# Attention and top-1 experts on one core: the first two pairs transposed on TensorE, a second token buffer, the gates' products moved to the score buffers

## The chip, the cores and the metric

The kernel runs on one core of one Trainium2 chip. The metric is the device time of one execution in microseconds. Before the change it was 905.83 us, the median of three runs (904.97 to 908.14).

## The reference

```python
scores = (q @ k.T) / sqrt(D) - log(S)          # per batch and head; B=8, H=12, S=448, D=64
attn   = sigmoid(scores) @ v
x      = attn, heads beside each other         # 3584 tokens x 768
logits = x @ w_gate                            # 768 x 8
expert = argmax(logits); gate = softmax(logits)[expert]
out    = gate * (relu(x @ w1[expert]) @ w2[expert])   # w1 768x1024, w2 1024x768
```

Everything is float32. The kernel splits the operands of the experts into a high and a low fp32r part and adds three products (high x high, high x low, low x high).

## The kernel before

**Attention** works on pairs of heads, six to a batch, 48 in all; two pairs run side by side, in seven steps each, which makes 168 steps. `scores(s)` puts the products of two pairs into two of four PSUM buffers (tag `sc`), `squash` turns each into `at` on ScalarE, and `weighted` adds the products with v into `av`, two buffers of its own. A pair's keys and queries are loaded by `load_pair` as 32 x 32 blocks and transposed by VectorE in `turn`, in the steps that `READY` names. The first two pairs are loaded and turned ahead of the loop, after `warm_up(WARM)`, 76 small matmuls on a constant.

**Experts.** When a batch's attention is done, its gate finds each token's expert and the expert that most of the batch's tokens chose. That expert is run over the whole batch as a block: `moe(b)` makes 288 matmuls, 144 with w1 (L208) into eight sums, then 144 with w2 (L229) into six, each sum in one of two PSUM buffers (tag `moe`). `hh` (ScalarE) and `hl` (VectorE, L214) are the two parts of a w1 sum after the relu; `ob` (L237, VectorE, then a multiplication by the gate on POOL, L239) is the transposed w2 sum. The weights are loaded by SP into a ring of five buffers (tag `wst`); ScalarE makes the high part and POOL subtracts it (`w1l`, `w2l`, L144).

**The interleaving.** One generator, `attention()`, goes through 185 steps and yields twice in each; from step `START` (33) on, each yield is followed by seven expert matmuls. So the order of the instructions on each engine is the order of the code. Two matmul steps of attention stand together in every even step, ahead of the first yield. In the second part of a step stands what the gate of the batch before has to do:

- a: `gate_a`, the product with the gate weights (`psg`), copied to `g16`
- b: four small transposes (`pl`), then a chain of VectorE operations to the one-hot rows `oh`
- c: the count of tokens for each expert (`pc`), then the expert's number and the gate values
- l: SP reads the expert's number into a register, from where the block's weights can be loaded
- d: the prefix sums (`pr`), VectorE's chain to the row numbers `si`, and four indirect DMAs of records on POOL (L355), for the tokens that chose another expert
- e: the gate values in rows (`gm`, `pg`, `gt`), needed at the block's first L239
- tokens: in six further steps, VectorE adds the two parts of x into `xf` (L398) and transposes it into `xt` (L399); after the third and the sixth, SP writes `xt` to `x_tok` with four DMAs (L403)

Steps a to e stand on neighbouring steps, with the exception that batch 0 has one free step behind b. The products psg, pl, pc, pr and pg are taken from `small_ps`, which shares the two `moe` buffers with the experts' sums. `xt` has one buffer.

**The tail.** After the loop, VectorE makes the list of the remaining work items (experts with records of other batches), `pli` (L675) turns it, and two loops with hardware counters run over the items. Between the parts of that list, `more(8)` puts eight of the last expert matmuls each. In an item, `AT` says after which matmul each split of the next item's weights is put.

Of the kernel before, what the change touches and what calls it, by code (L numbers as in the profile page):

```python
# [10 lines left out]
F32 = mybir.dt.float32  # L11
# [14 lines left out]
def tile_sigmoid_attention_top1_moe(  # L26
# [363 lines left out]
    def tokens(b, t):  # L390

        NB = S // 32
        n, t = divmod(t, KH)
        if t == 0:
            xts[b] = xtpool.tile([P, NB, KH, 32], F32, tag="xt", bufs=1, name=f"xt_{b}_{n}")
        xf = xtpool.tile([P, S], F32, tag="xf", bufs=1, name=f"xf_{b}_{n}_{t}")
        xh, xl = xch[b, n * KH + t]
        nc.vector.tensor_add(xf, xh.bitcast(F32), xl.bitcast(F32))  # L398
        nc.vector.transpose(xts[b][:, :, t, :], xf.rearrange("p (j s) -> p j s", s=32))  # L399
        if t == KH - 1:  # L400
            rows = x_tok[b * S : (b + 1) * S].rearrange("(j r) (i f) -> i r j f", r=32, i=4)
            for i in range(4):
                nc.sync.dma_start(  # L403
                    rows[i][:, :, n * KH * 32 : (n + 1) * KH * 32],
                    xts[b][32 * i : 32 * (i + 1)].rearrange("r j t s -> r j (t s)"),
                )

    def small_ps(b, name):

        return ps_moe.tile([P, 512], F32, tag="moe", name=f"{name}_{b}")  # L410

    att = ExitStack()
    xtpool = att.enter_context(tc.tile_pool(name="xtpool", bufs=2))
# [5 lines left out]

    DK = P // 2  # L420
    KC = S // DK
    ops = {}
    NG = B * NP
    OWN = [slice(h * D, (h + 1) * D) for h in range(2)]
# [5 lines left out]
    def load_pair(g):  # L430
        if g >= NG:
            return
        b, hp = divmod(g, NP)
        for nm, src in (("k", k), ("q", q)):
            t = apool.tile([P, S // 32, 32], F32, tag=nm + "n", bufs=4, name=f"{nm}n_{g}")
            eng = nc.scalar if g < Q_ACT and nm == "q" else nc.sync
            for h in range(2):
                for f in range(D // 32):
                    a = 2 * h + f
                    eng.dma_start(  # L440
                        t[32 * a : 32 * (a + 1)],
                        src[b, 2 * hp + h, :, 32 * f : 32 * (f + 1)].rearrange("(j r) s -> r j s", r=32),
                    )
            ops[g, nm + "n"] = t

    def load_values(g):
        if g >= NG:
# [16 lines left out]
    def warm_up(n):  # L464

        ps = ps_moe.tile([P, 512], F32, tag="moe", name="ps_warm")
        for _ in range(n):
            nc.tensor.matmul(ps[:, :P], ones, ones, start=True, stop=True)
# [4 lines left out]
    N_ST = NG // 2 * ST  # L473

    def squash(g, c, ps):
        at = apool.tile([P, S], F32, tag="at", bufs=10, name=f"at_{g}_{c}")
        nc.scalar.activation(at, ps[:, :S], AF.Sigmoid, bias=bias_s, scale=SCALE)  # L477
        ats[g, c] = at

# [32 lines left out]
                nc.vector.tensor_sub(xl, pv[:, :S], xh.bitcast(F32))  # L512
                xch[divmod(g, NP)] = (xh, xl)

    WARM, V_POOL, Q_ACT = 76, 10, 2
    START = 33
    PB = NP // 2 * ST
    MIX = (7, 7)

# [7 lines left out]
    def attention():  # L527

        order = ExitStack()
        order.enter_context(tc.manual_schedule())  # L530
        warm_up(WARM)
        load_pair(0)
        load_pair(1)
        for g in range(2):
            turn(g, "k")
            turn(g, "q")
            load_values(g)
        for g in (2, 3):
            load_pair(g)
# [3 lines left out]
        for s in range(N_ST + 11 + KD):  # L543
# [19 lines left out]
            if gb >= 0:  # L563
                b, r = divmod(gb, PB)
                r -= 3 if b == 0 else 2
                at = ("a", "b", None, "c", "l", "d", "e") if b == 0 else ("a", "b", "c", "l", "d", "e")
                what = at[r] if 0 <= r < len(at) else None
                if what == "a":
                    gate_a(b)
                elif what == "b":  # L570
                    pend_gate = gate_b(b)
                elif what == "c":
                    pend_gate = gate_c(b, *pend_gate)
                    gate_out[b] = pend_gate[0]
                elif what == "l":
                    load_regs(b)
                    if b == 0:
                        wts.ahead(0)
                elif what == "d":
                    gate_d(b, *pend_gate)  # L580
                elif what == "e":
                    gate_e(b)
                if 7 <= r < 7 + KD:
                    tokens(b, r - 7)
            yield s, MIX[1]
        order.close()

# [9 lines left out]
    def more(n):  # L597
        nonlocal left
        for _ in range(min(n, left)):
            next(mo)  # L600
            left -= 1
# [4 lines left out]
    for s, n in attention():  # L606
        if s >= START:
# [12 lines left out]
    AT = (  # L620
        (
            dict(zip((0, 1, 2, 3, 4, 12, 5, 6, 7, 8, 13, 14, 15, 16, 9, 10, 11, 17),
                     (33, 39, 45, 51, 57, 84, 102, 108, 114, 120, 126, 132, 138, 144, 150, 156, 162, 175))),
            (74, 90, 128, 168),
        ),
        (dict(zip((0, 1, 4, 5, 8, 9, 2, 3, 6, 7, 10, 11), (16, 20, 24, 28, 33, 42, 48, 54, 60, 66, 72, 78))), ()),
# [21 lines left out]
    nc.vector.tensor_scalar(cut(0), cut(0), float(P), None, op0=ALU.add)  # L648
    nc.vector.tensor_tensor(ek(4), ek(0), n_rec, op=ALU.is_lt)
    nc.vector.tensor_sub(few, few, big)  # L650
    more(8)
    for msk, cum in zip((big, few), rank):
        nc.vector.tensor_tensor_scan(cum, cut(3), msk, 0.0, op0=ALU.mult, op1=ALU.add)
    ends = rest.tile([P, 2], F32, name="ends")
# [2 lines left out]
    nc.vector.tensor_scalar(rank[1], rank[1], ends[:, 0:1], None, op0=ALU.add)  # L657
    for msk, cum in zip((big, few), rank):
        nc.vector.scalar_tensor_tensor(msk, cum, slot1, msk, op0=ALU.is_equal, op1=ALU.mult)
    more(8)  # L660
    nc.vector.tensor_add(big, big, few)
    prod = cut(8, 2).rearrange("p (a n) -> p a n", a=2)
    nc.vector.tensor_mul(
# [5 lines left out]
    ki = rest.tile([1, 2], I32, name="ki")  # L669
    nc.vector.tensor_scalar(ends[:, 0:1], ends[:, 1:2], -1.0, ends[:, 0:1], op0=ALU.add, op1=ALU.max)  # L670
    nc.vector.tensor_copy(ki, ends[0:1])
    more(8)
    pli = ps_x.tile([P, 512], F32, tag="px", name="pli")
    for a in range(2):
        nc.tensor.matmul(pli[0:1, a * P : (a + 1) * P], lf[:, a : a + 1], ident, start=True, stop=True)  # L675
# [237 lines left out]
```

## Time and profile before

| | before |
|---|---|
| median of three runs | 905.83 us |
| the profiled execution | 907.99 us |
| its span | 905.8 us |
| mean granted TensorE clock | 0.979 |
| TensorE (PE) busy | 859.9 us |
| VectorE, ScalarE, POOL busy | 376.4, 382.1, 413.5 us |
| bytes moved | 120.62 MB |

The times of the table's lower part belong to one profiled execution, on one core. The span goes from its first to its last recorded instruction. A group of instructions is written as engine, line, output <- inputs; a wait is put down to the instruction that ended it. These are the groups on which TensorE spends its time (busy us, mean ns of one, then idle time ahead of them and what ended it):

```profile
L503 PE MATMUL av<-at,vn 64*64 64x448 f32 x1344 | 157.8, 562 | 0.1
L490 PE MATMUL sc<-qt,kt 64*64 64x448 f32 x1344 | 152.2, 542 | 5.4 <-DVE qt L461 5.4
L208 PE MATMUL ps<-xh,w1h 128*128 128x448 f32 x384 | 144.2, 375 | 7.1 <-DVE hl L214 7.1
L229 PE MATMUL ps<-hh,w2h 128*128 128x448 f32 x384 | 143.6, 374 | 1.0 <-DVE g L260 1.0
```

### The profile page before, as it was taken

Reading aid. Unit: us, or ns where it says so; the run is one execution under the profiler, and the core shown is the slowest. Engines: PE = TensorE matmul, PEld = TensorE weight load, DVE = VectorE, ACT = ScalarE, POOL = GpSimd, SP = SyncE. Lnnn points to the kernel's source line nnn. Section 1 sums busy time; section 2 is a strip of 40 time slices with the busy share of each in tenths; the row PEclk is TensorE's granted clock in tenths of the full one; section 3 lists DMA queues with packets and bytes.
Section 4 is the critical chain, followed back from the end, with each engine's and each line's share of the span. In section 5 each row is a group of like instructions: output and inputs, shape, how many; then the busy total and the mean of one; then the engine's idle time right before and its main releaser. Section 6 shows DMA issues by size and latency. Waiting matters only on the chain.

```text
span 905.8 us, 15548 instructions
## 1 busy us (share of the span) xinstructions
PE 859.9 (95%) x5622; PEld 633.5 (70%) x5622; DVE 376.4 (42%) x729; ACT 382.1 (42%) x689; POOL 413.5 (46%) x377
## 2 busy tenths in 40 slices
PE   7989999999899999999999999999999999889986
PEld 4656766767577676677676676677676788779775
DVE  2356134732426225642434225532345136546354
ACT  3765434335243533354253543354344521324344
POOL 3115325823355415733475325732474358556240
PEclk8999999999999999999999999999999999999999
DMA  9878642876147843685248834676355306736614
GB/s 145 137 148 196 162 97 74 187 162 141 31 125 185 190 80 91 151 197 107 59 121 201 188 58 111 141 179 122 75 143 143 97 21 165 191 104 194 215 52 142
DMA packets 305644, 120.62 MB, mean 133 GB/s; under 512 B 215300, under 2 KB 300372, under 8 KB 305568
## 3 DMA queue, kind: packets, MB, share of 16 engines
q1 hardware_dynamic: 294368, 104.25, 49.8%
q0 software_dynamic: 7488, 14.93, 6.9%
q10 hardware_dynamic: 3712, 0.46, 0.4%
q8 instruction: 44, 0.72, 0.4%
q14 instruction: 32, 0.26, 0.1%
HBM read 97.55 MB, written 24.64 MB: 135 GB/s over the span
## 4 chain that ended last, share of the span: by engine, by line
PE 79%; DVE 7%; DMA 5%; POOL 3%; issue 2%; SPq 2%; ACT 1%; POOLq 0%; DVEq 0%; ACTq 0%
PE ps L208 23%; PE ps L229 22%; PE av L503 15%; PE sc L490 13%; PE ps L789 3%; PE psg L256 2%; DMA x_tok<-xt 1%; DMA qn<-in_q_dram 1%; DMA w2r<-in_moe_w_dram 1%; DVE xf L398 1%; POOL w1l L144 1%; DMA out_dram<-ob 1%; SPq L403 1%; DVE ob L237 1%; SPq L440 1%
## 5 line engine op out<-in xcount | busy, mean ns | idle before, releaser
L477 ACT ACTIVATE at<-sc,bias_s 128x448 f32<-128x448 f32 x336 | 187.1, 641 | 237.1 <-PE sc L490 236.8
L144 POOL TENSOR_TENSOR w2l<-wst,w2h 128x512 fp32r<-128x512 f32 x96 | 122.1, 1293 | 200.2 <-ACT w2h L143 153.3
L144 POOL TENSOR_TENSOR w1l<-wst,w1h 128x768 fp32r<-128x768 f32 x64 | 119.8, 1884 | 136.4 <-ACT w1h L143 129.7
L503 PE MATMUL av<-at,vn 64*64 64x448 f32 x1344 | 157.8, 562 | 0.1
L490 PE MATMUL sc<-qt,kt 64*64 64x448 f32 x1344 | 152.2, 542 | 5.4 <-DVE qt L461 5.4
L208 PE MATMUL ps<-xh,w1h 128*128 128x448 f32 x384 | 144.2, 375 | 7.1 <-DVE hl L214 7.1
L208 PE MATMUL ps<-xh,w1l 128*128 128x448 f32 x384 | 144.1, 375 | 1.9 <-POOL w1l L144 1.9
L229 PE MATMUL ps<-hh,w2h 128*128 128x448 f32 x384 | 143.6, 374 | 1.0 <-DVE g L260 1.0
L208 PE MATMUL ps<-xl,w1h 128*128 128x448 f32 x384 | 144.0, 375 | 0.0
L229 PE MATMUL ps<-hl,w2h 128*128 128x448 f32 x384 | 143.0, 372 | 0.0
L229 PE MATMUL ps<-hh,w2l 128*128 128x448 f32 x384 | 141.8, 369 | 0.0
L490 PEld LDWEIGHTS sc<-qt,kt 64*64 64x64 f32 x1344 | 77.1, 191 | 66.2 <-issue 55.4
L214 DVE SCALAR_TENSOR_TENSOR hl<-ps,hh 128x448 fp32r<-128x448 f32 x64 | 39.5, 617 | 183.6 <-ACT hh L213 183.6
L503 PEld LDWEIGHTS av<-at,vn 64*64 64x64 f32 x1344 | 49.5, 135 | 62.4 <-issue 52.1
L208 PEld LDWEIGHTS ps<-xh,w1h 128*128 128x128 f32 x384 | 73.7, 192 | 22.3 <-DVE hl L214 8.2
L229 PEld LDWEIGHTS ps<-hh,w2h 128*128 128x128 f32 x384 | 74.8, 195 | 15.6 <-issue 8.6
L208 PEld LDWEIGHTS ps<-xh,w1l 128*128 128x128 f32 x384 | 73.7, 192 | 16.2 <-issue 5.8
L208 PEld LDWEIGHTS ps<-xl,w1h 128*128 128x128 f32 x384 | 73.7, 192 | 14.0 <-issue 8.2
L229 PEld LDWEIGHTS ps<-hh,w2l 128*128 128x128 f32 x384 | 74.7, 195 | 11.4 <-issue 7.1
L229 PEld LDWEIGHTS ps<-hl,w2h 128*128 128x128 f32 x384 | 74.6, 194 | 9.8 <-issue 6.5
L143 ACT CAST w2h<-wst 128x512 fp32r<-128x512 f32 x96 | 57.6, 625 | 55.2 <-PE ps L229 51.0
L213 ACT ACTIVATE hh<-ps 128x448 fp32r<-128x448 f32 x64 | 35.2, 551 | 102.7 <-PE ps L208 102.7
(145 smaller groups left out, 891.4 us busy)
## 6 DMA issues: line engine op xcount, KB each, us to landing
wst<-in_moe_w_dram SPq DMA_DIRECT2D x64, 384.0 KB, 4.3
wst<-in_moe_w_dram SPq DMA_DIRECT2D x48, 512.0 KB, 4.6
kn<-in_k_dram SPq DMA_DIRECT2D x192, 56.0 KB, 3.9
x_tok<-xt SPq DMA_DIRECT2D x64, 168.0 KB, 3.9
out_dram<-ob POOLq DMA_DIRECT2D x96, 112.0 KB, 3.1
qn<-in_q_dram SPq DMA_DIRECT2D x184, 56.0 KB, 2.8
vn<-in_v_dram SPq DMA_DIRECT2D x76, 112.0 KB, 4.0
w1r<-in_moe_w_dram SPq DMA_DIRECT2D x12, 512.0 KB, 3.9
```

The source lines that it names most:

```text
L143: nc.scalar.copy(hi, st)
L144: eng.tensor_tensor(lo, st, hi.bitcast(F32), op=ALU.subtract)
L208: nc.tensor.matmul(ps[:, :S], a[:, ws], b_, start=(t == 0 and n == 0), stop=(t == KD - 1 and n == 2))
L213: nc.scalar.activation(hh[:, :S], ps[:, :S], AF.Relu)
L214: nc.vector.scalar_tensor_tensor(hl[:, :S], ps[:, :S], 0.0, hh[:, :S].bitcast(F32), op0=ALU.max, op1=ALU.subtract)
L229: nc.tensor.matmul(ps[:, :S], a, b_, start=(j == 0 and n == 0), stop=(j == KF - 1 and n == 2))
L237: nc.vector.transpose(ob[:, :, :, t], ps[:, :S].rearrange("p (j s) -> p j s", s=32))
L256: nc.tensor.matmul(psg[: 2 * E, :S], wgs[:, t], xch[b, t][n], start=(t == 0 and n == 0), stop=(t == KD - 1 and n == 1),)
L477: nc.scalar.activation(at, ps[:, :S], AF.Sigmoid, bias=bias_s, scale=SCALE)
L490: nc.tensor.matmul(ps[quarter(g, h), :S], ks, ops[g, "q"][OWN[h]], start=True, stop=True)
L503: nc.tensor.matmul(psv[g][OWN[h], :S], ops[g, "v"][rows, c, :], at[rows], start=(c == 0), stop=(c == KC - 1))
L789: nc.tensor.matmul(*a, **kw)
```

## The change

**First pairs.** `load_pair` isn't called for pairs 0 and 1. `first_pair` loads each as rows, 112 partitions of four tokens each, two DMAs for k (from SP) and two for q (from ScalarE's queue), into a buffer of the weights' ring. `first_turn` transposes it on TensorE, four transposes of 112 columns for each of k and q into a score buffer, and VectorE (k) or ScalarE (q) copies it out, with the tokens put back into their order. The two loads stand ahead of the warm-up, which has 50 matmuls instead of 76.

**Gates.** `small_ps` takes its buffer from the four score buffers. The steps are a, b, free, c, l, free, d, free, e for every batch, so a step for c, l and d of most batches and more for e lies later than before; the six token steps come one later.

**Token copies.** `xt` has two buffers; `at` has eight instead of ten.

**Start and tail.** `START` is 36 instead of 33. In the tail, three times 20 expert matmuls stand between the parts of the list instead of eight (the last `more(8)` stays), and the first five splits in `AT` stand three to five matmuls later.

```diff
@@ tokens @@
-            xts[b] = xtpool.tile([P, NB, KH, 32], F32, tag="xt", bufs=1, name=f"xt_{b}_{n}")
+            xts[b] = xtpool.tile([P, NB, KH, 32], F32, tag="xt", bufs=2, name=f"xt_{b}_{n}")
@@ small_ps @@
-        return ps_moe.tile([P, 512], F32, tag="moe", name=f"{name}_{b}")
+        return ps_sc.tile([P, 512], F32, tag="sc", name=f"{name}_{b}")
@@ load_pair @@
-            eng = nc.scalar if g < Q_ACT and nm == "q" else nc.sync
@@ new @@
+    PF = S // 4
+    def first_pair(g):
+        b, hp = divmod(g, NP)
+        t = wpool.tile([P, 1024], F32, tag="wst", bufs=RAWS_AHEAD, name=f"first_{g}")
+        tv = t[:PF].rearrange("p (n c h d) -> p n c h d", n=2, c=4, h=2)
+        for n, src in enumerate((k, q)):
+            for h in range(2):
+                eng = nc.scalar if n else nc.sync
+                eng.dma_start(tv[:, n, :, h], src[b, 2 * hp + h].rearrange("(p c) d -> p c d", c=4))
+        ops[g, "first"] = t
+
+    def first_turn(g):
+        t = ops.pop((g, "first"))
+        for n, nm in enumerate("kq"):
+            ps = score_tile(f"first_{g}_{nm}")
+            for c in range(4):
+                at = (4 * n + c) * P
+                nc.tensor.transpose(ps[:, c * PF : (c + 1) * PF], t[:PF, at : at + P], ident[:PF, :PF])
+            to = apool.tile([P, S], F32, tag=nm + "t", bufs=4, name=f"{nm}t_{g}")
+            tov, psv_ = to.rearrange("d (p c) -> d c p", c=4), ps[:, :S].rearrange("d (c p) -> d c p", c=4)
+            if nm == "k":
+                nc.vector.tensor_copy(tov, psv_)
+            else:
+                nc.scalar.copy(tov, psv_)
+            ops[g, nm] = to
@@ squash @@
-        at = apool.tile([P, S], F32, tag="at", bufs=10, name=f"at_{g}_{c}")
+        at = apool.tile([P, S], F32, tag="at", bufs=8, name=f"at_{g}_{c}")
@@ constants @@
-    WARM, V_POOL, Q_ACT = 76, 10, 2
-    START = 33
+    WARM, V_POOL = 50, 10
+    START = 36
@@ attention @@
+        for g in range(2):
+            first_pair(g)
         warm_up(WARM)
-        load_pair(0)
-        load_pair(1)
         for g in range(2):
-            turn(g, "k")
-            turn(g, "q")
+            first_turn(g)
             load_values(g)
...
-                at = ("a", "b", None, "c", "l", "d", "e") if b == 0 else ("a", "b", "c", "l", "d", "e")
+                at = ("a", "b", None, "c", "l", None, "d", None, "e")
...
-                if 7 <= r < 7 + KD:
-                    tokens(b, r - 7)
+                if 8 <= r < 8 + KD:
+                    tokens(b, r - 8)
@@ AT, first loop @@
-                     (33, 39, 45, 51, 57, 84, 102, 108, 114, 120, 126, 132, 138, 144, 150, 156, 162, 175))),
+                     (38, 43, 48, 54, 60, 84, 102, 108, 114, 120, 126, 132, 138, 144, 150, 156, 162, 175))),
@@ the list of items, three times @@
-    more(8)
+    more(20)
```

How the order of the instructions changes is seen at three places. First, TensorE after the warm-up (`sc_first_0_k` is the score buffer into which the keys of pair 0 are transposed; `sc_0_1` belongs to pair 0, step 1). Before:

```order
L468 MATMUL ps_warm_129<-ones_96 128x128
L490 MATMUL sc_0_0_261<-qt_0_228,kt_0_226 64x448 x2
L490 MATMUL sc_1_0_262<-qt_1_235,kt_1_233 64x448 x2
L490 MATMUL sc_0_1_271<-qt_0_228,kt_0_226 64x448 x2
L490 MATMUL sc_1_1_272<-qt_1_235,kt_1_233 64x448 x2
L503 MATMUL av_0_298<-at_0_0_267,vn_0_230 64x448 x2
```

After:

```order
L495 MATMUL ps_warm_139<-ones_96 128x128
L464 MATMUL sc_first_0_k_190<-ident_80,first_0_129 128x112 x4
L464 MATMUL sc_first_0_q_197<-ident_80,first_0_129 128x112 x4
L464 MATMUL sc_first_1_k_207<-ident_80,first_1_134 128x112 x4
L464 MATMUL sc_first_1_q_214<-ident_80,first_1_134 128x112 x4
L517 MATMUL sc_0_0_245<-qt_0_202,kt_0_195 64x448 x2
L517 MATMUL sc_1_0_246<-qt_1_219,kt_1_212 64x448 x2
L517 MATMUL sc_0_1_255<-qt_0_202,kt_0_195 64x448 x2
L517 MATMUL sc_1_1_256<-qt_1_219,kt_1_212 64x448 x2
L530 MATMUL av_0_282<-at_0_0_251,vn_0_204 64x448 x2
```

The last warm-up matmul is now followed by sixteen transposes in four buffers, and then by the same scores.

Second, POOL around the start of the last block, 7 (`ob_6_1` is the second output part of block 6, `w1l_7_0` the low part of block 7's first weights, `rec_7` the records of batch 7). Before:

```order
L144 TENSOR_TENSOR w2l_6_19_7759<-wst_6_13_7468,w2h_6_19_7758 128x512
L239 TENSOR_TENSOR ob_6_1_7644<-ob_6_1_7644,gt_6_7063 128x896
L244 DMA out_0_dram<-ob_6_1_7644 32x14x64 x4
L144 TENSOR_TENSOR w1l_7_0_7802<-wst_7_0_7777,w1h_7_0_7801 128x768
L351 IOTA rec_7_7831 128x4
L355 DMA recs_58<-rec_7_7831,si_7_7829 28672x2 x4
L144 TENSOR_TENSOR w1l_7_1_7852<-wst_7_1_7779,w1h_7_1_7851 128x768
```

After:

```order
L144 TENSOR_TENSOR w2l_6_19_7760<-wst_6_13_7480,w2h_6_19_7759 128x512
L351 IOTA rec_7_7787 128x4
L355 DMA recs_58<-rec_7_7787,si_7_7785 28672x2 x4
L239 TENSOR_TENSOR ob_6_1_7662<-ob_6_1_7662,gt_6_7084 128x896
L244 DMA out_0_dram<-ob_6_1_7662 32x14x64 x4
L144 TENSOR_TENSOR w1l_7_0_7818<-wst_7_0_7731,w1h_7_0_7817 128x768
L144 TENSOR_TENSOR w1l_7_1_7836<-wst_7_1_7733,w1h_7_1_7835 128x768
```

The records' four DMAs have moved from behind `ob_6_1`, its writes and `w1l_7_0` to a place ahead of all three.

Third, VectorE at the token copies of batch 7 (`xf_7_1_0` is the sum for the first of the second three, `hl_7_0` the low part of block 7's first two w1 sums). Before:

```order
L214 SCALAR_TENSOR_TENSOR hl_7_0_7931<-ps1_7_0_7907,hh_7_0_7930 128x448
L398 TENSOR_TENSOR xf_7_0_1_7944<-xh_43_7020,xl_43_7021 128x448
L399 STREAM_TRANSPOSE xt_7_0_7915<-xf_7_0_1_7944 128x14x32
L398 TENSOR_TENSOR xf_7_0_2_7961<-xh_44_7355,xl_44_7356 128x448
L399 STREAM_TRANSPOSE xt_7_0_7915<-xf_7_0_2_7961 128x14x32
L214 SCALAR_TENSOR_TENSOR hl_7_0_7931<-ps1_7_1_7940,hh_7_0_7930 128x448
L398 TENSOR_TENSOR xf_7_1_0_7992<-xh_45_7359,xl_45_7360 128x448
L399 STREAM_TRANSPOSE xt_7_1_7991<-xf_7_1_0_7992 128x14x32
L214 SCALAR_TENSOR_TENSOR hl_7_2_8001<-ps1_7_2_7977,hh_7_2_8000 128x448
```

After:

```order
L237 STREAM_TRANSPOSE ob_6_2_7809<-ps2_6_2_1_7848 128x448
L398 TENSOR_TENSOR xf_7_0_2_7906<-xh_44_7261,xl_44_7262 128x448
L399 STREAM_TRANSPOSE xt_7_0_7858<-xf_7_0_2_7906 128x14x32
L214 SCALAR_TENSOR_TENSOR hl_7_0_7925<-ps1_7_0_7898,hh_7_0_7924 128x448
L398 TENSOR_TENSOR xf_7_1_0_7939<-xh_45_7265,xl_45_7266 128x448
L399 STREAM_TRANSPOSE xt_7_1_7938<-xf_7_1_0_7939 128x14x32
L398 TENSOR_TENSOR xf_7_1_1_7956<-xh_46_7507,xl_46_7508 128x448
L399 STREAM_TRANSPOSE xt_7_1_7938<-xf_7_1_1_7956 128x14x32
L214 SCALAR_TENSOR_TENSOR hl_7_0_7925<-ps1_7_1_7934,hh_7_0_7924 128x448
```

The copies now stand further ahead: the second half's first two are in front of the second `hl_7_0`, where there was none before; `ob_6_2`, which was ahead of all of the copies, stands among them.

More of the change, by code (lines that the diff above doesn't have):

```diff
@@ L439, in load_pair @@
                     a = 2 * h + f
-                    eng.dma_start(
+                    nc.sync.dma_start(
                         t[32 * a : 32 * (a + 1)],
@@ L659, in tile_sigmoid_attention_top1_moe @@
         nc.vector.scalar_tensor_tensor(msk, cum, slot1, msk, op0=ALU.is_equal, op1=ALU.mult)
-    more(8)
+    more(20)
     nc.vector.tensor_add(big, big, few)
@@ L671, in tile_sigmoid_attention_top1_moe @@
     nc.vector.tensor_copy(ki, ends[0:1])
-    more(8)
+    more(20)
     pli = ps_x.tile([P, 512], F32, tag="px", name="pli")
```

## The prediction

> **What bounds the kernel.** I read the page first.
>
> ```profile
> PE 859.9 (95%) x5622; PEld 633.5 (70%) x5622; DVE 376.4 (42%) x729; ACT 382.1 (42%) x689; POOL 413.5 (46%) x377
> ```
>
> TensorE is busy for 860 of 905.8 us and no other engine for half. The change takes no expert or attention matmul away, so what it can win is TensorE's idle time and slow clock. The view of waits for PE gives the first:
>
> ```profile
> PE ps L208 <- DVE hl L214: 7.1, 3, 3.9
> PE sc L490 <- DVE qt L461: 5.4, 2, 5.1
> PE pg L378 <- DVE gm L374: 5.2, 5, 1.9
> PE pli L675 <- DVE lf L667: 4.0, 1, 4.0
> PE pc L302 <- DVE ob L237: 2.9, 2, 2.8
> ...
> PE ps L208 <- POOL w1l L144: 1.9, 1, 1.9
> ...
> PE pr L334 <- DVE pre L338: 1.1, 2, 0.5
> PE ps L229 <- DVE g L260: 1.0, 2, 0.5
> PE pc L302 <- DVE oh L289: 0.9, 1, 0.9
> PE pl L265 <- DVE g L260: 0.8, 1, 0.8
> PE pl L265 <- DVE ob L237: 0.5, 1, 0.5
> ```
>
> Columns: total us, times, longest. Nearly every wait is for VectorE, and nearly every one belongs to an edit. The second half of the price is the granted clock (the stretch, then busy times, then PEclk third from the end):
>
> ```profile
> 68.70:72.00 3.30, 3.30 (x24) 1.34 (x20) 3.23 (x6) 0.89 (x2) 2.39 (x4) 0.50 1.21 265
> 188.20:191.50 3.30, 3.30 (x11) 2.90 (x10) 3.27 (x7) 0.00 (x0) 1.57 (x1) 0.50 0.13 19
> 246.20:249.50 3.30, 3.30 (x18) 1.05 (x20) 2.19 (x11) 0.00 (x0) 2.89 (x5) 0.50 0.36 61
> 362.30:365.60 3.30, 3.30 (x16) 1.41 (x18) 0.00 (x0) 0.30 (x1) 2.67 (x4) 0.50 0.02 1
> 765.00:768.30 3.30, 3.30 (x11) 2.91 (x10) 3.30 (x1) 0.00 (x0) 3.00 (x3) 0.50 0.63 180
> 782.10:785.40 3.30, 3.30 (x11) 2.92 (x10) 1.44 (x3) 0.00 (x0) 0.00 (x0) 0.50 0.61 170
> 799.20:802.50 3.30, 2.96 (x9) 2.16 (x10) 0.98 (x4) 0.00 (x0) 0.00 (x0) 0.50 0.00 0
> ```
>
> Each of these 3.3 us stretches runs at half clock and lies just behind a wait. Sixteen attention matmuls show what one costs, cold and warm:
>
> ```profile
> 246.69 3.13 PE L503 MATMUL av<-at,vn 64*64 64x448 f32 x16
> ```
> ```profile
> 194.47 1.67 PE av L503 x16
> ...
> 197.64 5.86 PE ps L208 x28
> ...
> 206.67 5.86 PE ps L208 x28
> ```
>
> 3.4 x (1 - 1.67/3.13) = **1.6 us** a stretch. The same rows give an expert matmul 5.86/28 = 0.209 us, and a pair of steps with attention 206.67 - 197.64 = 9.03 us. Which waits pull the clock down:
>
> ```profile
> 67.95 0.28 PE L378 MATMUL pg<-gm,same 128*128 128x16 f32 x1 [1.64 <-DVE gm L374]
> ```
> ```profile
> 187.37 0.47 PE L208 MATMUL ps<-xh,w1h 128*128 128x448 f32 x1 [1.69 <-DVE hl L214]
> ```
> 1.64 and 1.69 us did; the others (1.9 to 4.0, the longest of their rows above) did too. The Trainium skill, page "TensorE: Matmul & The Clock Gate", section "Why this matters for your kernels", asks only for no idle gap above about 3 us; the trace disagrees, since 1.64 us sufficed, and I keep the 1.6 us. By the page's figure the sum below would be 4 x 1.6 = 6.4 us smaller, for the four stretches behind gaps under 3 us.
>
> **A, the start: 6.3 us.** Now pair 1 comes six us behind pair 0:
>
> ```profile
> 6.54 0.60 DVE L461 STREAM_TRANSPOSE qt<-qn 128x448 f32<-128x448 f32 x1
> ...
> 12.05 0.65 DVE L461 STREAM_TRANSPOSE kt<-kn 128x448 f32<-128x448 f32 x1 [4.91 <-DMA kn<-in_k_dram]
> ```
> ```profile
> 10.70:17.40 6.70, 4.12 (x24) 1.51 (x28) 1.82 (x3) 1.79 (x3) 1.64 (x5) 0.50 1.07 165
> ```
>
> TensorE is busy for the last 4.12 us of that stretch, from 13.3 to 17.4, all of it at half clock, which loses 4.1 x 0.47 = 1.9; some 0.4 us of scores was done before. So work starts, in full-clock time, at 13.3 + 1.9 - 0.4 = 14.8. After the change both pairs need 8 DMAs of 112 x 4 pieces, as many pieces as pair 0 had in its 8; pair 0 was ready at 6.5, pair 1 at 12.6, and these bound the landing. I take about 7, near the first, because pieces and not bytes set the time: 56 KB and 168 KB in equally many pieces land alike.
>
> ```profile
> kn<-in_k_dram SPq DMA_DIRECT2D x192, 56.0 KB, 3.9
> x_tok<-xt SPq DMA_DIRECT2D x64, 168.0 KB, 3.9
> ```
>
> The last four transposes cost 0.6 us warm and 1.1 cold (row below), the copy out of PSUM about 0.6 like VectorE's transposes above; the strided write is not in the trace, bounded by 0.6 and twice that. Scores run from about 8.5: 14.8 - 8.5 = 6.3, with ends 0.5 and 7.5. SP's issues for pairs 2 and 3 move ahead with it, and the shorter warm-up ends before the data lands, so it costs nothing.
>
> ```profile
> 846.93 1.12 PE L835 MATMUL ph<-ident,hf 128*128 128x128 f32 x4 [2.04 <-ACT hf L851]
> ```
>
> The Trainium skill's same page, section "Part 4: PE-mode transpose", says that transposes don't count as busy for the clock. No run here shows it; if it holds, the clock may fall at the start, which I price at one stretch among the rivals.
>
> **B, gates: 16.0 us.** Products a step further apart, in score buffers, concern the rows pg 5.2, pc 2.9 and 0.9, pr 1.1, ps<-g 1.0, pl<-ob 0.5: 11.6. I leave 0.4 of block 0's pg wait, where no expert matmul stands between. The row pl<-g, 0.8, stays: those two steps are still neighbours. Three stretches (68.7, 246.2, 362.3) go with them: 11.2 + 3 x 1.6 = 16.0. What hides VectorE's chain now is 28 expert matmuls (5.9 us and the attention between) instead of 14. What is late next is the ob transpose behind the chain, which its buffer's next group needs only 24 matmuls (5.0 us) later. New: a gate product holds a score buffer until VectorE has read it, and the scores behind it on TensorE queue. Seven expert matmuls, weighted sums and three score products (1.5 + 1.7 + 1.2 = 4.4 us) stand between, and the reads are the first things VectorE does with them. Bounds: nothing and, from the longest gate wait, 2.8 us a block. I take nothing.
>
> **C, token copies: 10.3 us.** The three ps<-hl waits come from VectorE standing before hl at the single token buffer:
>
> ```profile
> DVE xt L399 <- DMA x_tok<-xt: 41.2, 8, 10.8
> ```
>
> With two buffers the second half never waits for the first half's DMAs: 7.1 + 2 x 1.6 (188.2, 782.1) = 10.3. Five sixths of the 41.2 us were hidden anyway. SP's token DMAs keep their number. The score-result buffers fall from 10 to 8: at most three steps of two are alive, so that costs nothing.
>
> **D, routing of the tail: 5.6 us.** A step issues 14 expert matmuls, and there are 185 steps. So pli comes after (185 - 36) x 14 + 60 = 2146 expert matmuls instead of (185 - 33) x 14 + 24 = 2152, but the last token copy, in step 183 instead of 182, after (183 - 36) x 14 + 7 = 2065 instead of 2093, so VectorE has 81 matmuls instead of 59 between them: 22 x 0.209 = 4.6 us more, above the 4.0 waited. With the stretch at 799.2: 5.6. The split times in the item loop change nothing: the ph wait above hangs on hf, and stays, as do two waits near the end.
>
> **E, against: -1.8 us.** Block 7's record writes now stand ahead of ob_6_1 and w1l_7_0 on POOL:
>
> ```profile
> 750.18 0.19 PE L334 MATMUL pr<-lm,upper 128*128 128x32 bf16 x1
> ```
> ```profile
> 749.97 1.69 POOL L239 TENSOR_TENSOR ob<-ob,gt 128x896 f32<-128x896 f32 x1 [1.61 <-DVE pre L338]
> ...
> 752.20 0.17 DVE L349 TENSOR_SCALAR si<-sl 128x4 uint32<-128x4 f32 x1
> ...
> 752.84 2.54 POOL L244 DMA_DIRECT2D out_dram<-ob  x4 [1.17 <-issue]
> ```
> ```profile
> 755.38 1.85 POOL L144 TENSOR_TENSOR w1l<-wst,w1h 128x768 fp32r<-128x768 f32 x1
> 757.18 0.15 POOL L351 IOTA rec<- 128x4 uint32 x1
> ...
> 762.57 3.60 POOL L144 TENSOR_TENSOR w1l<-wst,w1h 128x768 fp32r<-128x768 f32 x2
> ```
>
> The pr product of step 176 stands after (176 - 36) x 14 + 7 = 1967 expert matmuls, 49 (10.2 us) ahead of block 7 at 7 x 288 = 2016. VectorE's chain from pr took 752.4 - 750.2 = 2.2 to si: -8.0. The writes took 762.6 - 757.2 = 5.4: -2.6. ob 1.7: -0.9. The out DMAs 2.5, with up to 1.2 ahead of them: +1.6 to +2.8. w1l 1.85: +3.5 to +4.7. TensorE wants it at its third matmul, +0.4. It waits about 3.7 in place of 1.9; the cold stretch at 765 stays.
>
> **F, against: -2.0 us.** In blocks 4 to 6 the writes now stand ahead of a w2l split that TensorE needs 25 matmuls after pr (in block 3's run pr comes 67 before its end and the split's use 42): 25/28 x 9.03 = 8.1 us. Chain, writes and split (1.85 x 512/768 = 1.2) need 2.2 + 5.4 + 1.2 = 8.8. Some 0.7 us late three times: -2.0; ends nothing and 3 x (1.6 + 1.6).
>
> **Sum.** 6.3 + 16.0 + 10.3 + 5.6 - 1.8 - 2.0 = 34.4. The profiled execution took 907.99 us with 905.8 of span, so it would take 873.6; it lies 2.2 above the median of the runs, 905.83, which becomes **871.4**.
>
> **Rivals.** Cold start: warm-up ends, TensorE idles for the last pair, and the transposes don't hold the clock; one more stretch and a landing a us or two later, 874 to 875. For: the half clock at 10.7 after a similar break. Against: work at 8.5 fills the next 3.4 us.
> POOL collisions: F's three waits reach 1.6 us and pull the clock, block 7 takes the upper end: 871.4 + 3 x 2.5 + 0.6 = 879.5.
> Token copies don't gain: an xf add of VectorE took 5 us beside POOL's splits (the two from 762.57),
>
> ```profile
> 763.30 5.00 DVE L398 TENSOR_TENSOR xf<-xh,xl 128x448 f32<-128x448 f32 x1
> ```
>
> so hl could stay late without the DMA: 871.4 + 10.3 = 881.7. Against: the copies also move 28 matmuls ahead, among ob transposes that have 24 matmuls of room.
> Short gaps don't pull the clock: the stretches behind waits under 3 us (68.7, 188.2, 246.2, 362.3) have another cause and stay, 871.4 + 4 x 1.6 = 877.8. That all four lie right behind a wait speaks against it. It is what the page's 3 us would make of this kernel.
> Better: F is nothing, block 7 waits less than now, the start lands as early as pair 0 did: 871.4 - 2.0 - 3.5 - 1.2 = 864.7.
> Slower than before: score buffers held by gate products while VectorE is behind. It decides where VectorE reads a product more than 4.4 us late in every block; it must then add 34.4/8 = 4.3 us a block, so reads 8.7 us late. Three blocks with xf adds could do that, not eight: 908 and more.
>
> **How the numbers follow.** Forecast 0.50 (867 to 876), cold start 0.13, POOL 0.12, copies 0.06, short gaps 0.03, better 0.12, slower 0.04. The range 861 to 884 leaves out some 0.15. A measurement of this kernel tells about 0.3% (2.7 us) from no change: faster 0.94, same 0.02, slower 0.04.
>
> **What would show it.** First scores at 8 to 9 us and no half clock before 20; no pg, pr, pc waits above 0.5; no xt wait for x_tok; no pli wait; a ps<-w1l wait of 3 to 4.5 us at block 7, and small ps<-w2l waits in blocks 4 to 6. Waits of sc for VectorE's reads of psg, pl, pc, pr or pg, or new waits of ps for ob, would make the forecast wrong.

## The result and the profile after

The changed kernel takes **893.39 us** (median of four runs, 891.24 to 895.21) against 906.99 before in the same series. The ratio is 0.9841, with a 95% interval of 0.9809 to 0.9873: 13.6 us faster, where 34 to 35 were forecast. The time lies above the range of 861 to 884.

The profiled execution took 891.24 us with a span of 889.1, at a mean granted clock of 0.986 (0.979 before). The page's row of the engines:

```profile
PE 852.7 (96%) x5612; PEld 633.4 (71%) x5612; DVE 385.6 (43%) x727; ACT 382.9 (43%) x691; POOL 413.8 (47%) x377
```

TensorE is busy 7.2 us less, which is mainly clock, since it does about the same work, and the gaps between its instructions sum up to 28.3 us (37.6 before). What it still waits for, in the view of waits (total us, times, longest):

```profile
PE pg L378 <- DVE gm L374: 7.2, 3, 3.7
PE ps L208 <- DVE hl L214: 6.7, 1, 6.7
PE ps L208 <- POOL w1l L144: 3.5, 2, 2.9
PE sc_first_k L464 <- DMA first<-in_k_dram: 3.2, 2, 2.6
...
PE pl L265 <- DVE g L260: 0.9, 1, 0.9
...
PE ps L229 <- POOL w2l L144: 0.3, 1, 0.3
```

Many rows are gone: pc, pr behind VectorE, pli, ps behind g, all three old waits for hl. But **pg has grown** from 5.2 to 7.2, and there is a new wait for hl, 6.7 us long. The chain of waits around block 3's pg shows the first of these (start, us, what):

```profile
351.26 0.03 DVE ob L237
...
351.83 0.60 DVE kt L488
352.43 2.52 DVE gm L374
...
355.09 0.37 PE pg L378 x2
```

gm, a product of 128 x 16 numbers, holds the chain for 2.5 us. In block 4 it takes 4.8. VectorE's timeline there, and POOL's beside it (start, us, what):

```profile
452.69 0.60 DVE L488 STREAM_TRANSPOSE kt<-kn 128x448 f32<-128x448 f32 x1
453.22 4.84 DVE L374 TENSOR_TENSOR gm<-gates,block 128x16 f32<-128x16 f32 x1
458.72 0.17 DVE L380 COPY gt<-pg 128x16 f32<-128x16 f32 x1 [0.66 <-PE pg L378]
```

```profile
452.64 3.74 POOL L144 TENSOR_TENSOR w2l<-wst,w2h 128x512 fp32r<-128x512 f32 x3
456.32 1.70 POOL L239 TENSOR_TENSOR ob<-ob,gt 128x896 f32<-128x896 f32 x1
```

gm ends at 458.06, when POOL's four operations end (458.02). The second wait, in VectorE's timeline at the end of the loop, and SP's before it:

```profile
761.50 0.58 DVE L214 SCALAR_TENSOR_TENSOR hl<-ps,hh 128x448 fp32r<-128x448 f32 x1
769.33 0.15 DVE L670 MEMSET xo<- 128x112 f32 x1 [7.24 <-DMA wst<-in_moe_w_dram]
...
774.04 0.61 DVE L214 SCALAR_TENSOR_TENSOR hl<-ps,hh 128x448 fp32r<-128x448 f32 x1
```

```profile
761.93 3.35 SPq L403 DMA_DIRECT2D x_tok<-xt  x4
765.53 8.86 SPq L136 DMA_DIRECT2D wst<-in_moe_w_dram  x3
```

VectorE stands before `xo`, the first write of the tail's list, for 7.2 us. The next hl stands behind it and behind 4.7 us of further list operations. The wait is put down to a weight load. But the token copies' DMAs are issued until 765.3, and with the median of 4.2 us to landing that the profile's page gives for `x_tok<-xt`, they would land at the same time.

### The profile page after: what moved, and what is told of

The parts are those of the page before. It is cut to its first block, busy times and chain, and to the rows that moved or that the text cites. A ratio compares the mean times of both kernels' runs of the same rounds, so it can differ in the third digit from the quotient of the medians.

```text
span 889.1 us, 15620 instructions
## 1 busy us (share of the span) xinstructions
PE 852.7 (96%) x5612; PEld 633.4 (71%) x5612; DVE 385.6 (43%) x727; ACT 382.9 (43%) x691; POOL 413.8 (47%) x377
## 4 chain that ended last, share of the span: by engine, by line
PE 85%; DVE 4%; issue 4%; DMA 3%; POOL 1%; SPq 1%; ACT 1%; POOLq 0%; DVEq 0%; ACTq 0%
PE ps L229 26%; PE ps L208 25%; PE av L530 14%; PE sc L517 13%; PE ps L815 3%; PE psg L256 2%; DVE xf L398 1%; DMA w2r<-in_moe_w_dram 1%; DVE gm L374 1%; DMA first<-in_k_dram 1%; DMA out_dram<-ob 1%; DVE w1l_item L144 1%; DMA wst<-in_moe_w_dram 0%; DMA w1r<-in_moe_w_dram 0%; SPq L403 0%
## 5 line engine op out<-in xcount | busy, mean ns | idle before, releaser
L530 PE MATMUL av<-at,vn 64*64 64x448 f32 x1344 | 153.4, 548 | 0.1
L229 PE MATMUL ps<-hh,w2l 128*128 128x448 f32 x384 | 144.1, 375 | 0.3 <-POOL w2l L144 0.3
L208 PEld LDWEIGHTS ps<-xh,w1l 128*128 128x128 f32 x384 | 73.2, 190 | 18.3 <-POOL w1l L144 6.2
L229 PEld LDWEIGHTS ps<-hh,w2h 128*128 128x128 f32 x384 | 75.4, 196 | 10.6 <-issue 6.5
L398 DVE TENSOR_TENSOR xf<-xh,xl 128x448 f32<-128x448 f32 x48 | 82.7, 1723 | 0.3
L229 PEld LDWEIGHTS ps<-hl,w2h 128*128 128x128 f32 x384 | 75.3, 196 | 10.1 <-issue 6.5
```

Of the source, the lines that this page charges most:

```text
L208: nc.tensor.matmul(ps[:, :S], a[:, ws], b_, start=(t == 0 and n == 0), stop=(t == KD - 1 and n == 2))
L229: nc.tensor.matmul(ps[:, :S], a, b_, start=(j == 0 and n == 0), stop=(j == KF - 1 and n == 2))
L530: nc.tensor.matmul(psv[g][OWN[h], :S], ops[g, "v"][rows, c, :], at[rows], start=(c == 0), stop=(c == KC - 1))
```

## The experiments

Times are medians; ratios are to the kernel before, with their intervals. The changed kernel's own is 0.9841 (0.9809 to 0.9873). Except where it says otherwise, each experiment starts from the changed kernel.

**1. gm earlier.** Theory: gm, issued directly ahead of pg, makes the waits on pg.

```diff
-                at = ("a", "b", None, "c", "l", None, "d", None, "e")
+                at = ("a", "b", None, "c", "l", "g", "d", None, "e")
...
+                elif what == "g":
+                    gate_g(b)        # gm alone; gate_e keeps pg and gt
```

> The changed kernel with one operation moved: gm, the product of gate values and block pattern, is issued in the free step between l and d, three steps ahead of pg, in place of directly ahead of it. Theory: the pg waits of the changed kernel (7.2 us, of which 3.25 in block 3 and 3.73 in block 4) come because gm stands behind the ob transpose in VectorE's queue, whose own sum TensorE has just finished, and because gm then takes 2.6 and 4.8 us beside POOL's multiplication of ob, in place of 0.13. Then the pg waits go, and with them the half-clock stretches at 356 and 458: 7.2 + 2 x 1.6 = 10.4 us less than the changed kernel, about 883. Rival: TensorE was held by the score buffers that gate products occupy, or VectorE's backlog comes to the next wait (scores, hl) whatever stands there: then a wait of about the same length shows up elsewhere in those two blocks and the time stays within 3 us of 893.

881.0 us, 0.9712 (0.9687 to 0.9737): 12.4 us less. No wait on pg is left in its view of waits, and no stretch at half clock between 17 and 738 us. The theory holds, and the gain is 2 us above the estimate.

**2. gm in place, one operand from PSUM.** This keeps gm's place in VectorE's queue and changes only from where it reads, at the price of one small product more on TensorE.

```diff
+        nc.tensor.matmul(pg[:, 64:68], ident, block, start=True, stop=True)
         nc.vector.tensor_tensor(
-            gm, gates[:, b].unsqueeze(2).broadcast_to(sh), block.unsqueeze(1).broadcast_to(sh), op=ALU.mult
+            gm, gates[:, b].unsqueeze(2).broadcast_to(sh), pg[:, 64:68].unsqueeze(1).broadcast_to(sh), op=ALU.mult
         )
```

> The changed kernel with gm left in its place, directly ahead of pg, but with one of its two operands read from PSUM (a small product on TensorE copies block there first). Theory: gm's 2.6 and 4.8 us are a block by POOL's multiplication and splits, which only operations that read both operands from SBUF or copy SBUF to SBUF suffer, as the durations in the traces so far say (hl and pre, one operand in PSUM, never take longer beside POOL). Then gm takes 0.2 us in all eight blocks and the pg waits of 3.25 and 3.73 fall to 0.7 to 1.3 (ob's and kt's transposes ahead of gm stay): some 5 us less waiting, with one or two half-clock stretches gone 885 to 888. Rival: the place in the queue alone makes the wait, or POOL slows VectorE whatever it reads: the waits stay near 3 us and the time near 893.

886.99 us, 0.9776 (0.9746 to 0.9806), within what was expected. The view of one tile (shortest, median, longest ns) for the changed kernel, then for this one:

```profile
L374 DVE TENSOR_TENSOR gm<-gates,block x8: 131/133/4842, 67.7 to 740.1; 128x16 f32<-128x16 f32 x8
```
```profile
L376 DVE TENSOR_TENSOR gm<-gates,pg x8: 131/171/172, 69.3 to 734.8; 128x16 f32<-128x16 f32 x8
```

The longest gm falls from 4842 to 172 ns, and the waits on pg from 7.2 to 2.4 us, none above 0.6. So the place in the queue costs 0.3 to 0.6 us a block, and POOL's work the rest. The gain is only half that of experiment 1: the 2.4 us on pg stay, and a wait for hl of 2.4 us has come at 754, where an xf that takes 4.0 us (from 751.0) stands ahead of hl. The Trainium skill, page "SBUF — State Buffer", section "SBUF: two separate sides", says that VectorE and GpSimd share a pair of SBUF ports under an exclusive lock, which a VectorE operation with two SBUF inputs needs too, so that the loser blocks fully. The trace agrees, and goes further: gm waits not for one operation but until POOL's run of four is over, whatever its own size.

**3. The list 20 matmuls later; 4. the list's first rows in memory of their own.**

```diff
+    more(20)
     nc.gpsimd.iota(ek(0), pattern=[[0, E], [TL, NK]], ...
```
```diff
+    g16_all = const.tile([P, NCH * P], F32, name="g16")
+    g16 = g16_all[: 2 * E]
...
+    cuts45 = small.tile([P, 2 * NI], F32, name="cuts45")
     def cut(n, w=1):
-        return scr[:, n * NI : (n + w) * NI]
+        where, n = (g16_all, n) if n < 4 else (cuts45, n - 4) if n < 6 else (scr, n)
+        return where[:, n * NI : (n + w) * NI]
```

> The changed kernel with 20 of the last expert matmuls put ahead of the first instructions of the tail's list (the writes to xo on POOL and VectorE). Theory: the 6.7 us wait of TensorE at 768 comes because xo lies in memory that xt had, so its first write waits for the last token copy's DMAs to x_tok, and hl of block 7 stands behind it in VectorE's queue; 20 matmuls are 4.2 us more of cover and one more hl ahead of it. Then this wait goes and the half clock behind it: 6.7 + 2.3 = 9 us less than the changed kernel, about 884. Rival: hl itself is late because VectorE is behind with the token copies (an xf add there took 8.3 us): then the wait stays at 5 us or more, and the time within 2 us of 893.

> The changed kernel with the first six rows of the tail's list in memory that was never part of the attention's pools; the rows from the scan on stay in xo. Nothing is moved. Theory: the 6.7 us wait of TensorE at 768 is VectorE's first write to xo, which waits for the release of the pool with xt, that is for the last token copy's DMAs. Then the first list operations run at once, and the wait moves behind the first 20 matmuls, to the scan: of the 6.7 us 0 to 3 are left there, and the time is 885 to 889. Rival: VectorE's backlog makes hl late: the wait stays at its place with 5 us or more, the time at 893.

The later list takes 889.32 us, 0.9821 (0.9796 to 0.9846), half of the gain that was expected: a wait for hl of 2.6 us stays, and the gather at the start of the tail, now later too, costs 1.2. With memory of its own the list takes 885.74 us, 0.9754 (0.9723 to 0.9784), as expected. Its rows of the view of waits for PE, and VectorE's first operation that still touches xo:

```profile
PE ps L209 <- DVE hl L215: 1.6, 1, 1.6
```
```profile
769.87 0.67 DVE L683 TENSOR_TENSOR_SCAN xo<-g,cuts 128x112 f32<-128x112 f32 x2 [2.65 <-DMA x_tok<-xt]
```

The wait has moved to the scan, and it now names the token copies' DMA. In experiments 1 and 5 the first write to xo names it too (6.2 and 11.0 us). That settles the cause: xo belongs to a pool that is opened where the pool with xt was closed, and its first write waits until xt's last DMA has landed.

**5. The last batch's records later.**

```diff
+                if b == B - 1 and r in (6, 12):
+                    what = "d" if r == 12 else None
```

> The changed kernel with step d of the last batch alone (prefix sums and the four record DMAs on POOL) six steps later. Theory: the wait for w1l at the start of block 7 (2.9 us, with half the clock behind it) comes from the record DMAs that now stand ahead of ob, its writes and w1l on POOL. Then it goes: 2.9 + 1.6 = 4.5 us less than the changed kernel, about 889. VectorE's xf add of 8.3 us there should get shorter too, without a change of the time. Rival: ob's multiplication, its output DMAs and three splits alone fill POOL there: then 1.5 us or more of the wait stays and the time is within 2 us of 893; or the records now hold up splits of block 7's weights, with new waits of 1 to 3 us for them.

901.08 us, 0.9941 (0.9919 to 0.9962): 7.7 us slower than the change. Half of each theory came true: the wait on w1l at the start of the block went, so the records did make it, and one of 1.5 us came behind their new place. What made the kernel slower was in neither. VectorE and POOL there:

```profile
740.07 5.98 DVE L374 TENSOR_TENSOR gm<-gates,block 128x16 f32<-128x16 f32 x1
```
```profile
740.70 5.31 POOL L144 TENSOR_TENSOR w1l<-wst,w1h 128x768 fp32r<-128x768 f32 x3
```

With the records gone, POOL goes from ob's output DMAs straight to three splits, and gm of block 7 ends with them (746.05): a wait on pg of 6.1 us takes the place of the one of 2.9 on w1l. It is a third showing of the block on gm, unasked. gm begins 0.6 us ahead of the splits, while POOL still issues those DMAs; what held it in that time no run tells. The list's wait grew to 8.7, too: SP's two weight loads ahead of the token copies' last DMAs took 9.9 us in place of 3.2.

**6. Three moves together; 7. gm, the list later and apart.**

> The three moves of the other kernels together: gm three steps ahead of pg, 20 matmuls ahead of the tail's list, the last batch's step d six steps later. If the three waits are independent the gains add up: 10.4 + 9 + 4.5 = 24 us less than the changed kernel, about 870. If one wait only hides the next, it is less than the sum of the three single gains by several us.

> gm three steps ahead of pg, 20 matmuls ahead of the list, and the list's first rows apart from xt's memory. The parts act at different waits: from gm_early's 881 the wait of 5.7 us at the list goes to 0 to 1, with its half clock (about 2 us): 873 to 876. If the list's operations on VectorE are held up by POOL's splits as in list_late, a wait of 2 to 3 us for hl stays and the time is 877 to 879.

882.32 us, 0.9738 (0.9712 to 0.9764): no better than gm alone. The wait of 5.4 us for hl in its trace is the list's again, although the list comes later: VectorE stands 8.4 us before the first write to xo, and SP's two weight loads ahead of the copies' last DMAs took 8.8 us (2.6 in experiment 1). And 878.8 us, 0.9691 (0.9664 to 0.9717), above the 873 to 876 of the theory. It lies in the range given for a wait for hl that stays, but that wait is gone; one of 2.2 us for the gathered rows of the tail takes its place.

**8. Pairs 2 and 3 held back.**

```diff
+        nc.sync.dma_start(mark, ops[1, "k"][0:1, 0:1])
         for g in (2, 3):
             load_pair(g)
```

> The changed kernel with a small DMA on SP, from pair 1's turned keys to memory, ahead of the loads of pairs 2 and 3, so that these start only when pair 1 is turned. Theory: pair 1's rows land at 9.7 us, not near 7, because 16 DMAs of pairs 2 and 3 share the DMA engines with them from 4 us on. Then pair 1 lands at 7 to 8 us, the scores start 2 us earlier, and the time is 891 to 892 or, where pairs 2 and 3 now come too late for step 7, 893 to 897 with a wait for their kt or qt. Rival: pair 1's own pieces set its landing (issues one behind the other on SP until 3.4 us, then 256-byte pieces): it lands at 9 us or later all the same.

895.67 us, 0.9866 (0.9837 to 0.9896). TensorE's timeline:

```profile
8.68 0.57 PE L465 MATMUL sc_first_k<-ident,first 112*128 112x112 f32 x4 [0.99 <-DMA first<-in_k_dram]
9.77 0.57 PE L465 MATMUL sc_first_q<-ident,first 112*128 112x112 f32 x4 [0.51 <-DMA first<-in_q_dram]
10.27 3.63 PE L518 MATMUL sc<-qt,kt 64*64 64x448 f32 x14
```

Scores start at 10.3 instead of 10.6, although pairs 2 and 3 load only afterwards. Over all traces with the new start they begin between 10.1 and 11.6, so the difference is no effect that can be told: the other pairs' loads are not what delays pair 1, and the rival holds. Holding them back only adds a wait for a qt at step 7 (1.4 us).

**9 to 12. One part undone at a time:** the first pairs as before; one token buffer (`bufs=1`); the gates on neighbouring steps (`"a", "b", "c", "l", "d", "e"`); their products in the experts' buffers (`ps_moe.tile`).

> The changed kernel with the first two pairs loaded and turned as before the change (blocks of 32 x 32, VectorE, 76 warm-up matmuls). The prediction's term A says that the new start is worth 6.3 us: then this kernel takes 899 to 900. The trace of the changed kernel says 2.2 us, since both pairs were ready at 10.6 us and not at 8.5: then 895 to 896, with the scores of steps 1 and up at 13 to 14 us again.

> The changed kernel with one token buffer again. The prediction's term C says that the second buffer took away waits of hl of 1.7, 1.5 and 3.9 us and two half-clock stretches: then VectorE waits for x_tok ahead of hl again in three or more blocks and the time is 900 to 904. If the waits of hl in the middle blocks came from an xf add beside POOL, and the one in block 7 from xo, the time stays within 3 us of 893.

> The changed kernel with the steps of the gates on neighbouring steps as before (a, b, c, l, d, e), their products still in the score buffers and the token steps where the change put them. By the prediction's term B the free steps hide VectorE's chain: then waits of TensorE for oh at pc (0.9) and for VectorE's first reads at pr (0.5) come back in several blocks, 2 to 4 us in all with at most one half-clock stretch, 895 to 899. pg's waits fall elsewhere: e now comes three steps earlier, beside other work of POOL. Rival: the buffers alone did it, and the spacing is worth nothing: within 2 us of 893.

> The changed kernel with the gates' products in the two buffers of the experts' sums again, a step apart as now. By the prediction's term B the rows that name ob or g go with the change of the buffer alone: then waits of ps for VectorE's g and of pc, pl and pg for ob come back, 4 to 5 us with one half-clock stretch, 897 to 900. Rival: with a step between them the products no longer meet a busy buffer, and the buffers are worth nothing: within 2 us of 893.

| undone | us | ratio to before (interval) | against the change |
|---|---|---|---|
| the start | 894.41 | 0.9859 (0.9829 to 0.9888) | +1.0 |
| second token buffer | 903.97 | 0.9953 (0.9927 to 0.9978) | +10.6 |
| spacing of the gates | 890.68 | 0.9841 (0.9797 to 0.9886) | none to be told |
| score buffers for products | 899.22 | 0.9909 (0.9879 to 0.9938) | +5.8 |

With one token buffer VectorE waits for the copies again (first row, waits for DVE), and one wait for hl in a middle block is back, of 4.2 us at 584 (second row, for PE; the other wait in it is the list's):

```profile
DVE xt L399 <- DMA x_tok<-xt: 52.0, 8, 10.3
```
```profile
PE ps L208 <- DVE hl L214: 10.4, 2, 6.3
```

The ten runs of this kernel fall into two groups, three at 898 to 899 us and seven at 903 to 906, and the trace is of one of the three. So it explains some 5 of the 10.6 us; what the seven slower runs wait for isn't shown.

With the products in the experts' buffers, gates and expert sums wait for each other again; some rows of its waits for PE:

```profile
PE pl L265 <- DVE hl L214: 2.2, 2, 1.1
PE psg L256 <- DVE hl L214: 1.4, 2, 1.1
...
PE ps L229 <- DVE rk L343: 0.7, 1, 0.7
```

With the gates on neighbouring steps no wait at pc or pr comes back, and none does with the old buffers and the new spacing either: for these rows each part suffices alone. For ps behind g and pl behind ob the buffers are needed. Beside them the spacing shows no worth in the time; its kernel has other waits, though (w2l 2.8 us, and pg 7.0 us in seven waits, the longest 1.8), so what it does by itself stays open.

**13. Both faults taken away; 14. the same with the records a step earlier.**

> The changed kernel with both faults of the forecast taken away and nothing else moved: gm three steps ahead of pg, and the list's first rows in memory apart from xt. If the wait on gm and the wait on xo are the whole of what the forecast missed behind the start, the two gains add up: single gains of 12.4 (gm) and 7.7 us (xo) give 873 to 874, near the forecast of 871.4 for the change. If a further wait comes to light behind them, as in the kernel with the list moved as well, the time stays at 877 to 880.

> The same with step d one step earlier in every batch, directly behind l, and gm one step ahead of pg. The record DMAs come 14 matmuls (some 4.5 us with the attention between, 2.9 at the end) earlier on POOL. Theory: then block 7's wait for w1l (3.4 us with its half clock) shrinks to below 1.5 us and the time is 2 to 4 us under the kernel without this move. Rival: the DMAs now stand ahead of a split of w2 of the block before, and that wait takes its place (2.8 us in the kernel with the gates on neighbouring steps): no change within 1.5 us.

875.09 us, 0.9675 (0.9647 to 0.9704), and 881.98, 0.9742 (0.9714 to 0.977). The first is 18.3 us under the change and 29.5 under the kernel before in its own series, with experiment 7 the fastest version; the two single gains, 12.4 and 7.7, nearly add up. The longest waits that it has left for the experts' operands:

```profile
PE ps L209 <- POOL w1l L145: 4.4, 2, 3.8
...
PE ps L209 <- DVE hl L215: 1.6, 1, 1.6
```

In the second, the records meet a split of w2 instead (a wait of 3.5 us at 728), as the rival had it. But a wait for hl of 4.8 us comes too, and the move costs 7 us, where the rival had no change.

## Why the prediction was wrong

Its terms against the two profiled executions, in us (907.99 to 891.24 is 16.8):

| term | forecast | in the traces |
|---|---|---|
| A, start | 6.3 | 2.2 |
| B, gates | 16.0 | 5.6 |
| C, token copies | 10.3 | 1.5 |
| D, list of the tail | 5.6 | 5.6 |
| E, block 7's records | -1.8 | -1.0 |
| F, w2l in blocks 4 to 6 | -2.0 | -0.3 |
| in no term | 0 | 3.2 |

**B failed at one step:** "What hides VectorE's chain now is 28 expert matmuls". That is true of pc and pr, whose inputs are made in an earlier step. It is not true of pg: gm is made in pg's own step, with no matmul between, however far e stands from d. I booked pg's 5.2 us among the waits that distance takes away, and I had not asked what made gm late. Its view before the change:

```profile
L374 DVE TENSOR_TENSOR gm<-gates,block x8: 131/132/1104, 67.7 to 753.4; 128x16 f32<-128x16 f32 x8
```

At the median it took 0.13 us, so where pg waited, gm was mostly late by its place in the queue; the one of 1.1 us stood beside POOL. The new places of e put it beside POOL's splits and multiplication, for 2.6 us in block 3 and 4.8 in block 4. The waits of the gates fell from 12.4 to 8.4, and one stretch at half clock fewer is left, not three. Of the rest, pc and pr would have gone with the distance alone or with the buffers alone (experiments 11 and 12).

**C was right about the token buffer and forgot the memory.** The three waits went, and undoing the buffer costs 10.6 us by medians. But the first write to xo hangs on the last copy's DMAs. Before the change 35 matmuls stood between that copy and the list, now 21, the same shift by one step that D is built on. I counted for D what comes behind the list's first write and not what the write itself waits for, although VectorE's timeline of before had it:

```profile
789.06 0.15 DVE L644 MEMSET xo<- 128x112 f32 x1 [1.64 <-DMA x_tok<-xt]
```

The new wait of 6.7 us and the half clock behind it (774.7 to 779.2, some 2.1 us) take nearly all of C back.

**A was mis-sized.** Scores start at 10.63, not at 8.5:

```profile
9.74 0.57 PE L464 MATMUL sc_first_k<-ident,first 112*128 112x112 f32 x4 [2.57 <-DMA first<-in_k_dram]
...
10.63 3.64 PE L517 MATMUL sc<-qt,kt 64*64 64x448 f32 x14
```

I took 7 us for the landing because equally many pieces had landed at 6.5. Pair 0's rows were there at 6.2, but pair 1's only at 9.7: with twice the bytes it took longer, and experiment 8 shows that the loads of pairs 2 and 3 are not to blame. What sets this landing, pieces, bytes or their order in the queues, no run tells apart. The first scores run at half clock (11.2 to 14.6), which was the rival "cold start"; in five of the experiments' traces (3, 5, 6, 7 and 10) the new start has no such stretch. The copies took 0.94 to 0.96 us each, inside my bounds of 0.6 and 1.2. At step 5 of the scores 2.2 us are left of the gain (21.03 before, 18.83 after); the run with the old start is 1.0 us slower by medians, within what can be told.

**D, E and F** held in kind: no wait on pli, one of 2.9 on w1l where I had 3.7, and one of 0.3 on w2l where I had three of 0.7. The 3.2 us in no term are for the most part the wait of ph, now 1.5 in place of 2.0, and the stretch behind it, which isn't there this time.

Of the rivals, "token copies don't gain" came nearest in time (881.7), through another mechanism. It rested on VectorE being held beside POOL, and I had that row (an xf of 5 us), but drew the conclusion only for hl. "POOL collisions" had the right engine, but priced its splits and not what it does to VectorE. The slower rival had no part in it: no score waited for a gate product to be read. With the two missed waits taken away (13), the kernel comes to 875.1, 3.7 from the forecast; A alone fell 4.1 short, so the other terms' errors about cancel there.

## What to carry to other kernels

More distance between two steps helps only what was already started in the first; a small operation issued directly ahead of its consumer is as late as its queue, and as late as another engine can make it. Before trusting such distance, look at an operation's longest duration beside its median: 4842 against 133 ns says that it is blocked, and by whom the other engines' timelines tell. And when a step is moved, look for what reuses its memory, not only for what reads its data: the first write to a new tile can wait for the last transfer out of an old one.

## What was not expected of the hardware

**Which operations POOL blocks.** Over the profile before, xf (two inputs from SBUF) took 0.58 us at the median without POOL's arithmetic beside it and 1.47, at most 6.68, with it. hl and the additions to pre (one input from PSUM) and the 32 x 32 transposes took the same in both cases. After the change one xf took 8.3 us.

**A wait's price in clock depends on where it falls.** The same wait on pg in block 3 (3.24 to 3.25 us) in three kernels, then the two stretches of 3.5 us behind it, with the granted clock third from the end; the changed kernel first, then the one with the later list, then the one with the later records:

```profile
355.50:359.00 3.50, 3.50 (x11) 3.14 (x11) 3.47 (x5) 0.00 (x0) 3.49 (x5) 0.56 1.16 257
359.00:362.50 3.50, 3.50 (x23) 2.41 (x26) 3.47 (x2) 0.00 (x0) 2.47 (x2) 0.95 0.71 168
```
```profile
354.50:358.00 3.50, 3.50 (x19) 3.34 (x20) 3.14 (x5) 0.00 (x0) 3.46 (x5) 1.00 1.18 254
358.00:361.50 3.50, 3.50 (x34) 2.00 (x36) 3.47 (x2) 0.00 (x0) 2.77 (x2) 1.00 0.71 166
```
```profile
354.00:357.50 3.50, 3.50 (x10) 3.20 (x11) 2.85 (x5) 0.00 (x0) 3.39 (x5) 0.50 1.11 246
357.50:361.00 3.50, 3.50 (x13) 3.14 (x13) 3.46 (x2) 0.00 (x0) 2.88 (x2) 0.64 0.67 136
```

It cost one stretch, none, and two. A wait of 1.64 us pulled the clock down before the change; one of 2.7 us on w1l in experiment 2 didn't. The Trainium skill's limit of about 3 us (page "TensorE: Matmul & The Clock Gate", section "Why this matters for your kernels") separates neither pair; no single length does in these runs.

The granted clock in the traces tells more. The stretches at half clock fill whole cells of a grid, 3.413 us each: in the changed kernel they begin at 355.91, 458.31, 748.45 and 772.34, which are 30, 85 and 7 cells apart. What decides is how long TensorE is idle within one cell. In the first kernel 2.6 of the 3.25 us fall into the cell that ends at 355.9, and the next one is at half clock. In the second an edge at 352.8 cuts the wait into 1.66 and 1.58, and nothing follows. In the third 2.4 fall ahead of the edge at 353.2 and 0.8 behind it, and the two cells from 353.2 are slow. The 1.64 us before the change lie in one cell; the 2.7 us of experiment 2 are cut into 1.3 and 1.4. Over all sixteen traces, from 20 to 864 us, no cell at full clock with less than 1.64 us idle was followed by a slow one, all 43 with more than 1.91 were, and of the 20 between 9 were.

So a slow cell has a fixed length, but whether a wait brings one depends on where the grid lies against the program, and the prediction took one for each of its waits. A single execution can't be held to that: the five runs of experiment 7 spread from 875.45 to 880.62 us, and the fastest and the slowest had granted clocks of 0.993 and 0.985.
